# Two-layer decode kernel: 384 more columns of W_q stay on chip, 384 more columns of V are lent out, two loads become one

## The chip, the cores and the metric

The kernel runs on one core of a Trainium2 chip. The metric is device time in microseconds: the median of repeated executions. One execution was also taken apart by the hardware profiler, and all rows below come from that one. A difference of 0.2% is 1.46 us here.

## The reference

Two identical layers run one after the other on a residual stream x of 4 rows and 640 columns (one new token for each of 4 sequences). Each layer is attention over a cache and then a gated MLP, each behind a layer norm:

```python
def attention(x):                       # 32 heads of 128, the last W = 1024 cache entries
    q = (x @ wq).reshape(B, 1, 32, 128)
    p = softmax(q . k_cache[:, :, -1024:, :] * 128 ** -0.5)
    return (p . v_cache[:, :, -1024:, :]).reshape(B, 1, 4096) @ wo

def mlp(x):                             # F = 1728
    gate, up = x @ W_gate, x @ W_up
    return (gate * (gate > 0) * up) @ W_down

x = x + attention(layernorm(x)); x = x + mlp(layernorm(x))     # layer 0
x = x + attention(layernorm(x)); x = x + mlp(layernorm(x))     # layer 1, same weights, same cache
```

Everything is float32. The host only cuts and reorders the arrays; all the arithmetic is on the chip.

## The kernel before

**Layout.** Every operand is laid out over 128 partitions, so that a "column" is one float on each partition (512 bytes in all). There are three long rows of columns in HBM: `heads` (255,744 columns: W_q, K, W_o and V of heads 0 to 26, in the order in which they are used), `kept` (47,360 columns: W_o, W_q, K and V of heads 27 to 31) and `mlp` (25,920 columns). One large buffer `store` (50,624 columns) takes the loads; a second, `first_q` (`HELD` = 4,288 columns), takes the first columns of `heads`, which are the start of W_q.

**What is loaded twice.** Both layers use the same weights and cache, but they do not fit on the chip. `heads` and `mlp` are loaded once in each layer. `kept` is loaded once, at the end of layer 0's attention, and stays for layer 1, which begins with its heads. `first_q` stays as well, so layer 1 loads `heads` from column `HELD` on.

**The plan.** Before any instruction is made, the list `plan` fixes for each load its columns and its place in `store` (`put`, `stretch`, and hand-written lists of sizes such as `gu`, `gu_end` and `wd`). Loads are all issued by SyncE (its queue is SP in the profile), at L216 and L221, strictly in the order of the plan. A load waits on the chip until the last instruction that reads its place in `store` has ended, and the next load waits behind it.

**Groups.** The heads are worked on in nine groups, 0 to 5 of four heads, 6 and 7 of three and 8 of two. Groups 7 and 8 are `kept`. In the loop of `attention`, the step of group g does, in this order on TensorE: the transposes of g's probabilities (L440 into `pp`), the end of group g-1 (L477), the scores of group g+1 (`ps`, L252 through `product`), the projection of group g-1 by W_o (`y`, L252) and the values of group g (`po`, L252). So in the step of group 6 the scores of group 7 stand ahead of the projection of group 5.

**Lent places.** While `kept` lies in `store`, layer 0's MLP still has to be loaded. Three pieces of `kept` are copied away by ScalarE, so that MLP columns can use their places: `AHEAD` (768 columns, into `probs`), `BACK` (1,600 columns, into idle PSUM columns of `ps`, `po` and `yy`) and `AWAY` (1,408 columns, into idle columns of `pp` and of the two `banks`). `BACK` comes back into `store` during layer 1's first scores (L428 to L430), `AWAY` at the end of layer 0's MLP (L610 to L612).

Of the kernel before, what the change touches and what calls it, by code (L numbers as in the profile page):

```python
# [13 lines left out]
B, D, H, DH, W, F = 4, 640, 32, 128, 1024, 1728  # L14
P = 128
KC = D // P
QUARTER = D // 4
# [34 lines left out]
GU0, GU = KC * 3 * P, KC * 4 * 256  # L52
WD0 = GU0 + 3 * GU
TAIL, WD1, WD = WD0 + D, WD0 + D + 2 * QUARTER, 4 * D
MLP = WD1 + 3 * WD
# [2 lines left out]

HELD = 4288
STORE = 50624
FRONT = KEPT * 2 * (D + KV)


AHEAD = KEPT * D, KEPT * D + 768
BACK = FRONT - 2 * KV - 1600, FRONT - 2 * KV
AWAY = BACK[0] - 1408, BACK[0]
HOME = 12992
FIRST, MOST = 32640, 16320  # L70
LAP = 3 * MOST + 1024
# [36 lines left out]
def decode_kernel(ctx: ExitStack, tc: tile.TileContext, x, source, sel, out):  # L108
    nc = tc.nc
# [10 lines left out]
    store = big.tile([P, STORE], F32, name="store")  # L120
# [3 lines left out]
    away = store[:, AWAY[0]:AWAY[1]]  # L124
# [43 lines left out]


    f, z, a, q, k = FRONT, STORE - D, AHEAD[0], AWAY[0], BACK[0]  # L170
    assert STORE - FRONT == 2 * 1280 + 64 + D
    gu = [(z, D), (f, 1280), (f + 1280, 1344), (a, 768), (k, 960), (k + 960, 640), (q, 1408)]
    gu_end = [(f, 1280), (f + 1280, 1280), (f + 2560, D)]
    wd = [(a, D), (k, 960), (k + 960, D), (q, 1280), *gu_end, (a, D), (k, D), (k + D, D)]
    lo = 0
    for to, n in gu + gu + gu_end + wd:
        put(0, "mlp", to, lo, lo + n)
# [2 lines left out]


    lo = HELD
    for to, n in (f, 1280), (f + 1280, 1280), (f + 2560, D + 64), (a, 768), (k, 1600):
        put(1, "heads", to, lo, lo + n)
        lo += n
    to = AHEAD[1]
# [14 lines left out]
    to = stretch(1, hi, last, 0)  # L201
    for lo, hi in (last, near(last + 12800)), (near(last + 12800), heads_end):
        to = put(1, "heads", to if to + hi - lo <= STORE else 0, lo, hi)
    cuts = [0, 7040, 12160, GU0 + 3 * GU, WD1 + WD, MLP - 4 * D, MLP - 2 * D, MLP - D, MLP]
    for lo, hi in zip(cuts, cuts[1:]):
        to = put(1, "mlp", to if to + hi - lo <= STORE else 0, lo, hi)

# [88 lines left out]

    ps = ps_s.tile([P, 2, 512], F32, name="ps")
    pp = ps_p.tile([P, 2, 512], F32, name="pp")
    parked = pp.rearrange("p j n -> p (j n)")[:, 256:896]
    po = ps_o.tile([P, 512], F32, name="po")  # L300
    nc.vector.memset(ps, 0.0)
    nc.vector.memset(po, 0.0)
# [113 lines left out]
    def scores(layer, g):  # L416
        n = len(HEADS[g])
        to = sc[g] = pp if layer and g == order[1][0] else ps
        for i, h in enumerate(HEADS[g]):
            for j in range(2):  # L420
                for b in range(B):
                    lo = (j * B + b) * 512
                    at = SIDE - 1 + SIDE * (B * i + b) - i
                    product(to[32 * b:32 * b + SIDE, j, :], qT[:, at:at + SIDE], *part(layer, "k", h, lo, 512),
                            start=i == 0, stop=i == n - 1, tile_position=(0, 32 * b))
                    part_done(layer, "k", h, lo, 512)
                    if to is pp and k0 + i * KV + lo < HOME + BACK[1] - BACK[0] <= k0 + i * KV + lo + 512:
                        nc.scalar.copy(store[:, HOME:HOME + 1024], ps.rearrange("p j n -> p (j n)"))  # L428
                        nc.scalar.copy(store[:, HOME + 1024:HOME + 1280], po[:, 256:])
                        nc.scalar.copy(store[:, HOME + 1280:HOME + 1600], yy[:, QUARTER:3 * QUARTER])  # L430
        nm[g] = small.tile([P, 1], F32, name="nm", bufs=1)
        nc.vector.tensor_reduce(nm[g], to.rearrange("p j n -> p (j n)"), axis=AX.X, op=ALU.max, negate=True)  # L432

# [8 lines left out]
    def values(layer, g, last=False):  # L442


        n = len(HEADS[g])
        for i, h in enumerate(HEADS[g]):
            t = pT[i % 2]
            to = t[:, GAP:].rearrange("p (c x) -> p c x", c=8)[:, :, :B]
            for j in range(2):
                nc.vector.tensor_copy(to[:, 4 * j:4 * j + 4], pp[:, j].rearrange("p (c x) -> p c x", c=4)[:, :, i:P:32])  # L450
            for c in range(8):
                a = c % 4
                at = GAP + SIDE * B * c - B * i
                product(po[32 * a:32 * a + SIDE * B], t[:, at:at + SIDE * B], *part(layer, "v", h, c * 512, 512),
                        start=i == 0 and c < 4, stop=i == n - 1 and c >= 4, tile_position=(0, 32 * a))
                part_done(layer, "v", h, c * 512, 512)
        if last:
            waits[0] = layer == 0
            fill(1, pp[:, 0])
        nc.scalar.copy(gates, po)  # L460
        if last and layer == 0:
            nc.scalar.copy(po[:, 256:], store[:, BACK[0] + 1024:BACK[0] + 1280])
            nc.scalar.copy(parked, away[:, :640])
            free(*BACK)

    def totals(g):
# [24 lines left out]
    def attention(layer):  # L491
        gs = order[layer]
        rstd = query(layer, gs[0], True, normalized())
        query_out(gs[0], rstd)
        query(layer, gs[1])
        query_turned(gs[0])
        go_on()
        query_out(gs[1], rstd)
        scores(layer, gs[0])
        query(layer, gs[2])  # L500
        softmax(gs[0])
        query_turned(gs[1])
        query_out(gs[2], rstd)
        for before, g, after, then in zip([None] + gs, gs, gs[1:] + [None], gs[2:] + [None] * 2):
            totals(g)
            turned()
            if layer == 0 and after is None:
                nc.scalar.copy(probs[:, QUARTER:QUARTER + 768], store[:, AHEAD[0]:AHEAD[1]])
                nc.scalar.copy(ps.rearrange("p j n -> p (j n)"), store[:, BACK[0]:BACK[0] + 1024])
                nc.scalar.copy(yy[:, QUARTER:3 * QUARTER], store[:, BACK[1] - 320:BACK[1]])  # L510
                free(*AHEAD)
            if before is not None:
                values_turned(before)
            if then is not None and before is not None:
                query(layer, then)
                query_out(then, rstd)
            if after is not None:
                scores(layer, after)
                softmax(after)
            else:  # L520
                table(AF.Sqrt)
            if then is not None:
                query_turned(then)

            if before is not None and not (layer == 0 and after is None):
                project(layer, before)
            values(layer, g, after is None)
        values_turned(gs[-1])
        if layer == 0:
            for i in range(2):  # L530
                nc.scalar.copy(banks[i][:, P:], away[:, 640 + 384 * i:1024 + 384 * i])
            free(*AWAY)
            project(layer, gs[-2])
        fill(1)
        project(layer, gs[-1], True)

    def forward(layer):
# [69 lines left out]
        down(0)  # L607
        hidden(2, h)
        if layer == 0:
            nc.scalar.copy(away[:, :640], parked)  # L610
            for i in range(2):
                nc.scalar.copy(away[:, 640 + 384 * i:1024 + 384 * i], banks[i][:, P:])  # L612
            live[AWAY[0]:AWAY[1]] = [True] * 1408
        down(1)
        down(2, last=True)

# [62 lines left out]
```

## Time and profile before

| | |
|---|---|
| median of 3 runs | 731.91 us (731.81 to 732.6) |
| the profiled execution, its own time | 731.96 us |
| its span, first to last instruction | 730.2 us |
| TensorE busy, mean granted clock | 443.9 us (61%), 0.82 |
| VectorE, ScalarE busy | 76.1 us, 54.5 us |
| queue of the loads, share of the 16 DMA engines | 99.0% |
| moved | 311.17 MB, 426 GB/s over the span |

The span is the part of an execution that the trace covers; the execution's own time is 1.76 us longer. The share of a DMA queue is the time that its packets took, as a share of 16 engines' span. The granted clock is that of TensorE, as a share of 2.4 GHz, and it has two levels, 1.0 and 0.5.

### The profile page before, as it was taken

The numbers are of one execution on the slowest core, as the hardware profiler recorded it, in microseconds if no ns is written. First come the engines' busy times: TensorE is split into PE (matmuls) and PEld (weight loads), VectorE is DVE, ScalarE is ACT, GpSimd is POOL, SyncE is SP. The second block draws the span as 40 slices with busy tenths as digits, with TensorE's granted clock in tenths as the row PEclk, the third lists the DMA queues.
The fourth block names the chain that finished last, engine by engine and source line by source line (L and its number), as shares of the span: only waits on it lengthen the run. The fifth ranks groups of instructions, "written<-read, shape, count | busy, mean of one in ns | idle before, by whom it ended". The sixth has DMA issues, their size and how long they took to land.

```text
span 730.2 us, 8291 instructions
## 1 busy us (share of the span) xinstructions
PE 443.9 (61%) x3776; PEld 147.1 (20%) x3776; DVE 76.1 (10%) x277; ACT 54.5 (7%) x101; POOL 0.2 (0%) x4
## 2 busy tenths in 40 slices
PE   0845665654646565519878896365656556555576
PEld 0211111111111111103344241021111112111233
DVE  1110001010010101002111211001010010101011
ACT  0200000000000000000412210000000000000110
POOL 0000000000000000000000000000000000000000
PEclk9976788877777776759999999677777778878899
DMA  9999999999999999999999999999999999999996
GB/s 409 446 393 446 442 439 437 419 436 439 432 428 429 417 456 424 443 413 429 420 409 396 432 429 446 442 436 424 432 431 443 436 430 423 446 432 432 416 427 286
DMA packets 13290, 311.17 MB, mean 426 GB/s; under 512 B 1476, under 2 KB 1732, under 8 KB 6984
## 3 DMA queue, kind: packets, MB, share of 16 engines
q1 hardware_dynamic: 13104, 310.56, 99.0%
q8 instruction: 29, 0.48, 0.2%
q10 hardware_dynamic: 152, 0.09, 0.1%
q14 instruction: 5, 0.04, 0.0%
HBM read 310.57 MB, written 0.08 MB: 425 GB/s over the span
## 4 chain that ended last, share of the span: by engine, by line
DMA 77%; PE 20%; another core or an unknown queue 1%; issue 1%; DVE 0%; ACT 0%; SPq 0%; DVEq 0%; ACTq 0%
DMA store<-in_heads 60%; PE ps L252 9%; DMA store<-in_kept 8%; DMA store<-in_mlp 8%; PE po L252 5%; PE m L252 2%; PE y L252 1%; PE pp L252 1%; PE pp L440 1%; PE m L411 1%; PE m L477 0%; PE m L468 0%; PE m L349 0%; PE y L379 0%
## 5 line engine op out<-in xcount | busy, mean ns | idle before, releaser
L252 PE MATMUL po<-store,pT 128*16 128x512 f32 (+1 forms) x1026 | 156.0, 716 | 122.4 <-DMA store<-in_heads 117.0
L252 PE MATMUL ps<-store,qT 128*4 128x512 f32 (+3 forms) x996 | 151.0, 687 | 109.5 <-DMA store<-in_heads 87.9
L252 PEld LDWEIGHTS po<-store,pT 128*16 128x16 f32 x1026 | 34.4, 110 | 230.8 <-issue 110.7
L252 PEld LDWEIGHTS ps<-store,qT 128*4 128x4 f32 x996 | 30.0, 93 | 213.2 <-DMA store<-in_heads 98.9
L432 DVE TENSOR_REDUCE nm<-ps 128x1 f32<-128x1024 f32 x17 | 20.8, 1225 | 241.0 <-PE ps L252 241.0
L436 ACT ACTIVATE probs<-ps,nm 128x1024 f32<-128x1024 f32 x17 | 18.9, 1114 | 327.2 <-DVE nm L432 327.2
L252 PE MATMUL m<-store,xT 128*32 128x512 f32 (+4 forms) x150 | 29.0, 580 | 10.5 <-DMA store<-in_heads 10.3
L450 DVE COPY pT<-pp 128x16 f32<-128x16 f32 x128 | 17.2, 169 | 137.5 <-PE po L252 137.5
L460 ACT COPY gates<-po 128x512 f32<-128x512 f32 x18 | 10.5, 586 | 268.3 <-PE po L252 268.3
L252 PE MATMUL y<-store,oT 128*4 128x160 f32 x514 | 22.8, 309 | 9.6 <-DMA store<-in_heads 8.4
L440 PE MATMUL pp<-sel_sb,probs 128*128 128x128 f32 x144 | 20.4, 289 | 0.0
L470 DVE RECIPROCAL r<-m 128x16 f32<-128x16 f32 x18 | 4.6, 258 | 132.2 <-PE m L468 132.2
L440 PEld LDWEIGHTS pp<-sel_sb,probs 128*128 128x128 f32 x144 | 17.9, 151 | 0.0
L252 PE MATMUL pp<-store,xT 128*32 128x256 f32 (+3 forms) x172 | 14.3, 417 | 4.7 <-DMA store<-in_mlp 4.7
L252 PEld LDWEIGHTS y<-store,oT 128*4 128x4 f32 x514 | 12.7, 88 | 17.3 <-DMA store<-in_heads 8.8
L404 DVE TENSOR_SCALAR gates<-m,rstd 128x512 f32<-128x512 f32 (+2 forms) x18 | 12.4, 690 | 24.3 <-PE m L252 24.0
L477 PE MATMUL m<-sel_sb,gates 128*128 128x128 f32 x72 | 11.8, 291 | 1.1 <-ACT gates L460 1.1
L411 PE MATMUL m<-sel_sb,gates 128*128 128x128 f32 x64 | 12.4, 318 | 0.0
L327 PE MATMUL y<-probs,sel_sb 4*4 4x160 f32 x8 | 0.7, 445 | 18.0 <-DMA sel_sb<-in_sel 18.0
L411 PEld LDWEIGHTS m<-sel_sb,gates 128*128 128x128 f32 x64 | 7.7, 157 | 19.2 <-issue 18.8
L252 PE MATMUL y<-store,gates 128*4 128x160 f32 x192 | 9.6, 299 | 2.4 <-DMA store<-in_mlp 2.2
L252 PEld LDWEIGHTS m<-store,xT 128*32 128x32 f32 x150 | 6.2, 116 | 22.0 <-DMA store<-in_heads 12.5
(79 smaller groups left out, 143.5 us busy)
## 6 DMA issues: line engine op xcount, KB each, us to landing
store<-in_heads SPq DMA_DIRECT2D x17, 7936.0 KB, 45.8
store<-in_heads SPq DMA_DIRECT2D x2, 8160.0 KB, 44.5
store<-in_heads SPq DMA_DIRECT2D x2, 8128.0 KB, 35.9
store<-in_heads SPq DMA_DIRECT2D x2, 7968.0 KB, 36.3
store<-in_heads SPq DMA_DIRECT2D x1, 8096.0 KB, 26.3
store<-in_heads SPq DMA_DIRECT2D x1, 7424.0 KB, 44.1
store<-in_heads SPq DMA_DIRECT2D x1, 7360.0 KB, 35.4
store<-in_heads SPq DMA_DIRECT2D x1, 7168.0 KB, 35.1
```

The lines of the kernel that those rows point to most:

```text
L252: nc.tensor.matmul(out[:, a:z], by, t[rows, p:p + z - a], start=start and not a, stop=stop and z == n, **how)
L327: nc.tensor.matmul(y[32 * g:32 * g + B], ident[:B, :B], probs[:B, g * QUARTER:(g + 1) * QUARTER], start=True, stop=True, tile_position=(0, ...
L404: nc.vector.tensor_scalar(gates[:, :len(HEADS[g]) * P], qp.pop(g), rstd, SCALE, op0=ALU.mult, op1=ALU.mult)
L411: nc.tensor.transpose(qt[:, i], gates[:, i * P:(i + 1) * P], ident)
L432: nc.vector.tensor_reduce(nm[g], to.rearrange("p j n -> p (j n)"), axis=AX.X, op=ALU.max, negate=True)
L436: nc.scalar.activation(probs, sc.pop(g).rearrange("p j n -> p (j n)"), AF.Exp, bias=nm.pop(g), accum_out=sums[g])
L440: nc.tensor.transpose(pp[:, c // 4, c % 4 * P:c % 4 * P + P], probs[:, c * P:(c + 1) * P], ident)
L450: nc.vector.tensor_copy(to[:, 4 * j:4 * j + 4], pp[:, j].rearrange("p (c x) -> p c x", c=4)[:, :, i:P:32])
L460: nc.scalar.copy(gates, po)
L470: nc.vector.reciprocal(r[g], so.rearrange("p (b i) -> p i b", b=B)[:, :SIDE])
L477: nc.tensor.transpose(ot[:, 127 * b:127 * b + P], gates[:, b * P:(b + 1) * P], ident)
```

## The change

`HELD` goes from 4,288 to 4,672 columns and `store` from 50,624 to 50,240, so the sum stays. `AWAY` grows by 384 columns at its lower end. Its columns now go to 768 idle columns of `pp` (640 before), 768 of the two `banks` (as before) and 256 of the two `pT` tiles. `pT` has to hold zeros between the probabilities that it carries, so GpSimd clears its first 128 columns after the copy back. The pieces of `BACK` change places among their three homes. The MLP's loads in layer 0 are cut otherwise (same number of columns), and layer 1's first 12,160 MLP columns come in one load, not in 7,040 and 5,120.

```diff
-HELD = 4288
-STORE = 50624
+HELD = 4672
+STORE = 50240
 FRONT = KEPT * 2 * (D + KV)
 AHEAD = KEPT * D, KEPT * D + 768
 BACK = FRONT - 2 * KV - 1600, FRONT - 2 * KV
-AWAY = BACK[0] - 1408, BACK[0]
+AWAY = BACK[0] - 1792, BACK[0]
...
-    gu = [(z, D), (f, 1280), (f + 1280, 1344), (a, 768), (k, 960), (k + 960, 640), (q, 1408)]
-    gu_end = [(f, 1280), (f + 1280, 1280), (f + 2560, D)]
-    wd = [(a, D), (k, 960), (k + 960, D), (q, 1280), *gu_end, (a, D), (k, D), (k + D, D)]
+    gu = [(z, D), (f, 1152), (f + 1152, 1088), (a, 768), (k + 448, 1152), (k - D, 1088), (q, 1152)]
+    gu_end = [(f, 1408), (f + 1408, 1472), (k - 512, 320)]
+    wd = [(a, D), (k, 960), (k + 960, D), (q, 1280), (f, 1280), (f + 1280, 1280), (f + 2560, 320), (k, 320), (a, D),
+          (k + 320, D), (k + 960, D)]
...
     lo = HELD
-    for to, n in (f, 1280), (f + 1280, 1280), (f + 2560, D + 64), (a, 768), (k, 1600):
+    for to, n in (f, 1280), (f + 1280, 1280), (f + 2560, 320), (a, 768), (k, 1600):
...
-    cuts = [0, 7040, 12160, GU0 + 3 * GU, WD1 + WD, MLP - 4 * D, MLP - 2 * D, MLP - D, MLP]
+    cuts = [0, 12160, GU0 + 3 * GU, WD1 + WD, MLP - 4 * D, MLP - 2 * D, MLP - D, MLP]
...
-    parked = pp.rearrange("p j n -> p (j n)")[:, 256:896]
+    parked = pp.rearrange("p j n -> p (j n)")[:, 256:]
...
-            nc.scalar.copy(parked, away[:, :640])
+            nc.scalar.copy(parked, away[:, 1024:])
...
-                nc.scalar.copy(banks[i][:, P:], away[:, 640 + 384 * i:1024 + 384 * i])
+                nc.scalar.copy(banks[i][:, P:], away[:, 256 + 384 * i:640 + 384 * i])
+            for i in range(2):
+                nc.scalar.copy(pT[i][:, :P], away[:, P * i:P * i + P])
...
-            nc.scalar.copy(away[:, :640], parked)
+            nc.scalar.copy(away[:, 1024:], parked)
             for i in range(2):
-                nc.scalar.copy(away[:, 640 + 384 * i:1024 + 384 * i], banks[i][:, P:])
-            live[AWAY[0]:AWAY[1]] = [True] * 1408
+                nc.scalar.copy(away[:, 256 + 384 * i:640 + 384 * i], banks[i][:, P:])
+                nc.scalar.copy(away[:, P * i:P * i + P], pT[i][:, :P])
+                nc.gpsimd.memset(pT[i][:, :P], 0.0)
+            live[AWAY[0]:AWAY[1]] = [True] * (AWAY[1] - AWAY[0])
```

The plan is worked out from these numbers, so sizes and places of loads move elsewhere too. First, SP's queue at the end of layer 0's attention, before: the last loads of `heads` and the first of `kept` (columns are the second number).

```order
L221 DMA store<-in_heads 128x14336
L221 DMA store<-in_heads 128x14720
L221 DMA store<-in_heads 128x14848
L221 DMA store<-in_kept 128x12288
L221 DMA store<-in_kept 128x8192
L221 DMA store<-in_kept 128x6656
L221 DMA store<-in_kept 128x5632
```

The same place after the change:

```order
L222 DMA store<-in_heads 128x14336
L222 DMA store<-in_heads 128x14208
L222 DMA store<-in_heads 128x14848
L222 DMA store<-in_kept 128x12288
L222 DMA store<-in_kept 128x8192
L222 DMA store<-in_kept 128x6656
L222 DMA store<-in_kept 128x5632
```

The second load shown is 512 columns shorter. In both kernels it begins at place 20,736 of `store` and ends with column 240,896 of `heads`; its last place is 35,456 before and 34,944 now. The loads of `kept` keep sizes and places.

Second, ScalarE at the end of layer 0's attention, before: the copies that lend places out (`po`, `pp`, `m` are PSUM; `m` is `banks`).

```order
L460 COPY gates<-po 128x512
L462 COPY po<-store 128x256
L463 COPY pp<-store 128x640
L531 COPY m_109<-store 128x384
L531 COPY m_110<-store 128x384
L357 COPY probs<-y 128x160
```

After the change:

```order
L461 COPY gates<-po 128x512
L463 COPY po<-store 128x256
L464 COPY pp<-store 128x768
L532 COPY m_109<-store 128x384
L532 COPY m_110<-store 128x384
L534 COPY pT_98<-store 128x128
L534 COPY pT_99<-store 128x128
L358 COPY probs<-y 128x160
```

One copy is 128 columns longer and two of 128 columns are new; two such also follow the copies back at the end of layer 0's MLP.

Third, the end of SP's queue, before:

```order
L221 DMA store<-in_heads 128x12672
L221 DMA store<-in_mlp 128x7040
L221 DMA store<-in_mlp 128x5120 x2
L221 DMA store<-in_mlp 128x3520
L221 DMA store<-in_mlp 128x2560
```

After the change:

```order
L222 DMA store<-in_heads 128x12672
L222 DMA store<-in_mlp 128x12160
L222 DMA store<-in_mlp 128x5120
L222 DMA store<-in_mlp 128x3520
L222 DMA store<-in_mlp 128x2560
```

The first two loads of the second MLP are one. Elsewhere one small load is new, so the number of loads into `first_q` and `store` stays at 90.

## Rows read from the trace of the kernel before

**Rows 1.** The page: DMA busy share in 40 slices, and the loads' queue.

```profile
DMA  9999999999999999999999999999999999999996
...
q1 hardware_dynamic: 13104, 310.56, 99.0%
```

**Rows 2.** Windows: length, busy (instructions) by engine PE to POOL, PEclk, DMA share, GB/s.

```profile
3.00:200.00 197.00, 108.16 (x743) 32.14 (x746) 16.84 (x56) 11.32 (x19) 0.00 (x0) 0.80 1.01 435
...
450.00:696.00 246.00, 135.64 (x1015) 40.14 (x1017) 19.42 (x78) 11.03 (x18) 0.00 (x0) 0.78 1.00 433
```

**Rows 3.** The chain that ended last, its end: start, length, what.

```profile
695.92 30.69 DMA store<-in_mlp
...
726.65 0.50 PE y L252 x8
```

**Rows 4.** Timeline of SP, five short stretches: start and length of the issue.

```profile
0.73 0.37 SPq L216 DMA_DIRECT2D first_q<-in_heads  x1
...
298.10 0.33 SPq L221 DMA_DIRECT2D store<-in_kept  x1
...
301.46 0.33 SPq L221 DMA_DIRECT2D store<-in_kept  x1
...
380.80 0.33 SPq L221 DMA_DIRECT2D store<-in_mlp  x1
...
392.11 0.33 SPq L221 DMA_DIRECT2D store<-in_heads  x1
```

**Rows 5.** DMA issues at 0.73, 298.10, 301.46 and 377.51: size, us to landing.

```profile
first_q<-in_heads SPq DMA_DIRECT2D x1, 2144.0 KB, 7.5
...
store<-in_kept SPq DMA_DIRECT2D x1, 4096.0 KB, 37.5
...
store<-in_kept SPq DMA_DIRECT2D x1, 3328.0 KB, 42.0
...
store<-in_mlp SPq DMA_DIRECT2D x1, 640.0 KB, 6.6
```

**Rows 6.** The chain that ended last, 323 to 346 us and before 396.

```profile
325.66 7.96 PE ps L252 x48
...
333.99 1.20 PE y L252 x32
...
388.48 7.07 DMA store<-in_mlp
```

**Rows 7.** DMA queues, packets begun at 0.7 to 1.7 and 1.7 to 2.7 us.

```profile
q10 hardware_dynamic: 3, 0.01, 6.9%
...
q1 hardware_dynamic: 16, 0.27, 105.2%
```

**Rows 8.** DMA packets begun at 332.90 to 333.85 us.

```profile
DMA packets 16, 0.33 MB, mean 343 GB/s; under 512 B 4, under 2 KB 4, under 8 KB 4
```

**Rows 9.** ScalarE's groups by form: busy us, mean ns of one, idle before.

```profile
L531 ACT COPY m<-store 128x384 f32<-128x384 f32 x2 | 0.9, 472 | 0.0
...
L463 ACT COPY pp<-store 128x640 f32<-128x640 f32 x1 | 0.7, 688 | 0.0
```

**Rows 10.** Timeline of TensorE, 707 to 726 us: start, length, what.

```profile
707.41 1.18 PE L252 MATMUL po<-store,xT 128*32 128x128 f32 x27 [0.25 <-DVE xT L363]
...
709.14 2.37 PE L252 MATMUL pp<-store,xT 128*32 128x256 f32 x40
...
716.39 4.05 PE L252 MATMUL pp<-store,xT 128*32 128x256 f32 x40 [2.25 <-DMA store<-in_mlp]
...
721.23 1.27 PE L252 MATMUL y<-store,gates 128*4 128x160 f32 x32
```

**Rows 11.** Windows, 717 to 721 us, columns as in rows 2.

```profile
717.00:719.00 2.00, 2.00 (x24) 1.27 (x20) 0.00 (x0) 0.00 (x0) 0.00 (x0) 0.50 0.98 419
719.00:721.00 2.00, 1.98 (x31) 0.76 (x24) 0.10 (x1) 0.37 (x1) 0.00 (x0) 0.72 1.00 419
```

**Rows 12.** DMA issues at 672.69 us: size, us to landing.

```profile
store<-in_mlp SPq DMA_DIRECT2D x1, 2560.0 KB, 37.5
```

More of the change, by code (lines that the diff above doesn't have):

```diff
@@ L170, in decode_kernel @@
     f, z, a, q, k = FRONT, STORE - D, AHEAD[0], AWAY[0], BACK[0]
-    assert STORE - FRONT == 2 * 1280 + 64 + D
-    gu = [(z, D), (f, 1280), (f + 1280, 1344), (a, 768), (k, 960), (k + 960, 640), (q, 1408)]
-    gu_end = [(f, 1280), (f + 1280, 1280), (f + 2560, D)]
-    wd = [(a, D), (k, 960), (k + 960, D), (q, 1280), *gu_end, (a, D), (k, D), (k + D, D)]
+    assert STORE - FRONT == 2 * 1280 + 320
+    gu = [(z, D), (f, 1152), (f + 1152, 1088), (a, 768), (k + 448, 1152), (k - D, 1088), (q, 1152)]
+    gu_end = [(f, 1408), (f + 1408, 1472), (k - 512, 320)]
+    wd = [(a, D), (k, 960), (k + 960, D), (q, 1280), (f, 1280), (f + 1280, 1280), (f + 2560, 320), (k, 320), (a, D),
+          (k + 320, D), (k + 960, D)]
     lo = 0
@@ L427, in scores @@
                     if to is pp and k0 + i * KV + lo < HOME + BACK[1] - BACK[0] <= k0 + i * KV + lo + 512:
-                        nc.scalar.copy(store[:, HOME:HOME + 1024], ps.rearrange("p j n -> p (j n)"))
-                        nc.scalar.copy(store[:, HOME + 1024:HOME + 1280], po[:, 256:])
-                        nc.scalar.copy(store[:, HOME + 1280:HOME + 1600], yy[:, QUARTER:3 * QUARTER])
+                        nc.scalar.copy(store[:, HOME + 576:HOME + 1600], ps.rearrange("p j n -> p (j n)"))
+                        nc.scalar.copy(store[:, HOME:HOME + 256], po[:, 256:])
+                        nc.scalar.copy(store[:, HOME + 256:HOME + 576], yy[:, QUARTER:3 * QUARTER])
         nm[g] = small.tile([P, 1], F32, name="nm", bufs=1)
@@ L461, in values @@
         if last and layer == 0:
-            nc.scalar.copy(po[:, 256:], store[:, BACK[0] + 1024:BACK[0] + 1280])
-            nc.scalar.copy(parked, away[:, :640])
+            nc.scalar.copy(po[:, 256:], store[:, BACK[0]:BACK[0] + 256])
+            nc.scalar.copy(parked, away[:, 1024:])
             free(*BACK)
@@ L508, in attention @@
                 nc.scalar.copy(probs[:, QUARTER:QUARTER + 768], store[:, AHEAD[0]:AHEAD[1]])
-                nc.scalar.copy(ps.rearrange("p j n -> p (j n)"), store[:, BACK[0]:BACK[0] + 1024])
-                nc.scalar.copy(yy[:, QUARTER:3 * QUARTER], store[:, BACK[1] - 320:BACK[1]])
+                nc.scalar.copy(ps.rearrange("p j n -> p (j n)"), store[:, BACK[1] - 1024:BACK[1]])
+                nc.scalar.copy(yy[:, QUARTER:3 * QUARTER], store[:, BACK[0] + 256:BACK[0] + 576])
                 free(*AHEAD)
```

## The prediction

> **What bounds the kernel now.** I read the page first: the 16 DMA engines show 9 in 39 of 40 slices, and the queue of the loads alone fills 99.0% of them [rows 1]. The windows say at what rate: 433 to 435 GB/s at a share of 1.00 or more, while TensorE is busy for about half of the same stretches [rows 2]. The chain that ended last closes with a load that lands at 726.61 us (695.92 + 30.69) and one short group of matmuls behind it [rows 3]. So the span is the time in which the engines move 311 MB, plus a start and an end of a few us. A byte less is worth its time at 434 GB/s. TensorE, ScalarE and VectorE matter only where a load is issued so late that the queue runs dry, for with the engines full everywhere else such time is never made up.
>
> So for each load I compared two times: when it is issued, and when the load before it lands. Most have 15 us or more between them. The tightest that I found before is the first small load of layer 1, issued at 392.11 while the load ahead lands at 388.48 + 7.07 = 395.55 [rows 4, 6]: 3.1 us of queue are left when its issue ends.
>
> **The bytes saved.** Layer 1 starts loading `heads` at column 4,672, not 4,288. That is 384 columns x 512 bytes = 196,608 bytes, and at 434 GB/s 0.45 us. The kept columns of layer 0 are only moved from one load into another. The number of loads is the same, so what each row of a load costs beyond its bytes stays.
>
> **The load that now comes late.** `store` got shorter by 384 and the plan cut one load of layer 0 by 512 columns (14,720 to 14,208). It still ends with column 240,896 of `heads`, now at place 34,944. W_o of head 20, the first head of group 5, is columns 238,976 to 239,616, so it ends 1,280 places ahead of that: it lies at 33,536 to 34,176 before, and at 33,024 to 33,664 now. The load of 6,656 `kept` columns (V of group 7) goes to 26,880 to 33,536 in both. Before, it just misses W_o, and its last reader is an early V; now its last 512 places are still W_o of head 20, and it has to wait for the fourth matmul of group 5's projection. That projection stands behind the scores of group 7 on TensorE.
>
> What this costs is read at one place. Before, this load (3,328 KB) is issued at 301.46, and the 4,096 KB load ahead of it at 298.10 lands 37.5 us later, at 335.6; the late one itself lands at 343.5 [rows 4, 5]. The chain shows group 7's scores at 325.66, released by the landing of their K, and the projection from 333.99 [rows 6]. The bytes up to here are the same, so these times stay. The 16 matmuls are 32 records in 1.20 us, and the first head's are done about 0.4 us in: the issue moves from 301.5 to 334.4 us. Nothing can be issued meanwhile, since SP is in order and every later load stands behind it; the only data left in the queue are the 4,096 KB load's.
>
> How long the engines then stand still has to be bounded, as no row before shows a dry queue in the middle:
> - *Start of a load into an empty queue.* The first load is the nearest case. Issued at 0.73, it has no packet by 1.7, and 16 packets (one an engine) begin from 1.7 to 2.7 us [rows 4, 7]: 1.0 to 1.9 us after the start of the issue, 1.5 in the mean. For an issue at 334.4 the rows begin from 335.4 to 336.3, in the mean at 335.9.
> - *Where the engines would have been.* They do not finish a load together. In 0.95 us from 332.90 on 12 large packets begin and make up 0.33 MB, 27 KB each [rows 8]: that is the row length of the late load (26.6 KB), not of the one ahead (32.8 KB). So most engines are in it by 333 us. I take 333.1 as the mean.
> - *From above:* 336.3 less 332.2, some 4.1 us. *From below:* by landings, which the last engine sets. The first load lands 7.5 us after its issue [rows 5], and its 2,195,456 bytes take 5.06 us at 434 GB/s, so 2.4 us come on top. Issued at 334.4, 3,407,872 bytes (7.85 us) land at 344.7 instead of 343.5: 1.2 us.
>
> I take the mean over the engines, 335.9 - 333.1 = 2.8 us, since each engine has the same rows to move afterwards and the last of 16 to finish is hardly the one that was last here.
>
> A rule of the skill speaks for less. The Trainium skill ("DMA: Bandwidth & Descriptors", Latency and other measured facts) gives a DMA issued from SP about 600 ns to its first byte. By that, as an estimate, the stream would go on at 335.0, 1.9 us would be lost, and the time would be 733.4. The first load's packets, at 1.0 us and later, do not agree [rows 7].
>
> **The other edits.** ScalarE's copies while lending: 128 more columns in `pp` and two copies of 128. By the rows for 384 columns (472 ns) and 640 columns (688 ns) [rows 9], 128 columns cost some 0.11 us more in a copy and a copy of 128 some 0.25 us: 0.6 us in all, and the two loads that wait for these copies come up to 1.0 us later than before. They have about 7 us of queue ahead of them, as the small MLP loads land 7 us after issue [rows 5, 6]; if that cover were gone, the price would be 1.0 us. The same copies back, and GpSimd's clearing, end several us before layer 1's layer norm or its first values need them. In layer 0's MLP one load of 320 columns now waits for the first matmuls of the last gate tile. The load behind which it stands is at the place of the one that lands at 377.51 + 6.6 = 384.1, and its issue falls where 380.80 stands now [rows 4, 5]: 3 us of queue are left, about the tightest margin of before, so nothing is lost, and if its queue ran dry too, some tenths. Columns that fall in two loads split a few matmuls; TensorE has room.
>
> **The joined load.** It waits for the same values as the second of the two before (issued at 672.69, over 20 us ahead) [rows 12], so the queue does not notice. But TensorE may start the second MLP only when all 12,160 columns are there: where that load landed before, 672.69 + 37.5 = 710.2, and not at 707.41 [rows 10, 12]. On the clock of before, 1.3 us of the first gate tile, 0.5 of layer-norm matmuls and three tiles of 2.37 with 0.5 between them end at 719.6. An idle stretch of 2.25 us made TensorE drop to 1.2 GHz: the granted clock is 0.50 at 717 to 719 and 0.72 over the next 2 us, and the tile that ran in it took 4.05 us [rows 10, 11]. Now the idle stretch is about 3 us; a like drop costs 1.7 us, so the last tile ends at 721.3. Then 0.8 + 3 x 1.27 us of W_down follow, to 726.0, and the last load lands at 726.6. The cover is 0.6 us; it is hidden.
>
> **Sum.** The profiled execution's own time is 731.96 us (span 730.2 and 1.76 around it), 0.05 over the median. 731.96 + 2.8 - 0.45 = 734.3 us.
>
> **The rivals.**
> - *The queue dries up for less.* Only the last engine of the late load counts (1.2 us), or all engines start as soon as the first one did (335.4 - 333.1 = 2.3 us). For it: the end of the span is also a last engine's. Against it: the last here had no reason to be last at the end. 731.96 + 1.2 - 0.45 = 732.7, up to 733.8. The rule of the skill named above lies in between.
> - *No dry queue, not slower.* TensorE would have to reach head 20's projection 2 us sooner, before 332 us, less the time to start. Then only the bytes count: 731.96 - 0.45 = 731.5. The scores run 7.96 us behind a landing that the change does not touch [rows 6], which speaks against it. The same result comes if the saved bytes are all and the overlap of 512 places was misread.
> - *The joined load shows at the end.* If TensorE stays at 1.2 GHz longer than one such stretch, its work passes the last landing. A second stretch costs 1.7 us, of which 0.6 are covered: 1.1 more. With all four tiles at 1.2 GHz (2.6 and three of 4.05 us) they end at 726.5 and W_down at 731.1, 3.9 us behind the end of before. It comes on top: 735.4 to 738.2.
>
> **How the numbers follow.** The forecast has a chance of 0.69 at 734.3 us, by the bounds 1.2 and 4.1 at most 732.7 to 735.6. The smaller dry time has 0.16, no dry queue 0.08, the joined load on top 0.07. With 0.2% (1.46 us, about what a measurement tells from no change) slower begins at 733.37. The forecast is over it for 0.63, the smaller dry time for 0.04, the last rival for 0.06, together 0.73. Faster by over 0.2% needs 1 us more than the bytes give: 0.03. The rest, 0.24, is the same. The range reaches from 732.4 to 735.6: it leaves out the case without a dry queue and most of the last rival.
>
> **What would show it.** In the trace after, the 3,328 KB load is issued near 334.4 us with a projection matmul (`y`) as what it waited for, and lands some 10 us later, at 344.7 or after, not 42.0. The DMA share falls in the slice around 335, and all behind it is later by 2 to 3 us until layer 1's loads give 0.45 back. The MLP of layer 1 begins right with the landing of the joined load, and the last group of matmuls still waits for the last load. I would be wrong if that issue stands near 301 us, if the queue stays full at 335, or if TensorE ends later than 0.6 us behind the last landing.

## The result, and the profile after

The changed kernel takes 735.03 us in the median of 6 runs (734.12 to 735.96), against 732.09 us for the kernel before beside it: a ratio of 1.0039, 95% interval 1.0027 to 1.0051. It is slower by 2.9 us, 0.4%. The profiled execution took 735.43 us with a span of 733.6; the one of before, 731.96 and 730.2.

The page of the kernel after: the DMA busy share and the rate in 40 slices of 18.3 us, and the queue of the loads.

```profile
DMA  9999999999999999998999999999999999999996
GB/s 420 393 443 444 436 441 433 409 443 434 437 447 422 409 447 444 426 428 354 417 419 389 417 426 462 429 437 422 430 444 436 430 428 438 432 432 429 430 423 276
...
q1 hardware_dynamic: 13104, 310.37, 98.6%
```

Beside [rows 1] one slice of the share has an 8, and it is the one in which the rate falls to 354 GB/s: the 19th, 330 to 348 us. The bytes went from 310.56 to 310.37 MB. Far from that place the rate is that of before; windows of after, to be read beside [rows 2]:

```profile
3.00:200.00 197.00, 105.67 (x741) 30.82 (x744) 16.86 (x56) 11.25 (x19) 0.00 (x0) 0.80 1.01 435
450.00:696.00 246.00, 143.74 (x1043) 42.25 (x1041) 21.18 (x85) 12.23 (x20) 0.00 (x0) 0.76 1.00 434
```

SP's timeline of after, two short stretches; the first two loads answer to 298.10 and 301.46 in [rows 4]:

```profile
298.24 0.33 SPq L222 DMA_DIRECT2D store<-in_kept  x1
...
334.56 0.33 SPq L222 DMA_DIRECT2D store<-in_kept  x1
```

The view of waits of after, SP from 297 to 340 us (what it waited for: us in all, times, longest), and three lines of the chain that ended last, in order of time:

```profile
SPq L222 <- PE y L253: 36.0, 1, 36.0
```

```profile
325.73 8.01 PE ps L253 x48
333.75 0.37 PE m L412 x2
334.11 1.20 PE y L253 x32
```

DMA issues of after at 298.24 and at 334.56: size, us to landing.

```profile
store<-in_kept SPq DMA_DIRECT2D x1, 4096.0 KB, 37.5
...
store<-in_kept SPq DMA_DIRECT2D x1, 3328.0 KB, 11.7
```

So the load of 3,328 KB waits 36 us for a projection matmul, is issued 33.1 us later than before and lands at 346.3 (334.56 + 11.7) instead of 343.5. The load ahead of it has landed at 335.7. What the engines did meanwhile stands in the windows, here the same four of before and then of after (columns as in [rows 2]). A load is moved in rows, one packet for each partition (a "row" from here on is such a packet); a window counts a row whole where it begins, so a share can be over 1.00, and the 0.08 below means that two rows begin from 333 to 335 us while earlier ones still run.

```profile
331.00:333.00 2.00, 2.00 (x20) 0.39 (x16) 0.00 (x0) 0.00 (x0) 0.00 (x0) 1.00 1.14 486
333.00:335.00 2.00, 2.00 (x42) 0.95 (x34) 1.30 (x3) 0.00 (x0) 0.00 (x0) 1.00 0.97 419
335.00:337.00 2.00, 2.00 (x28) 0.59 (x24) 0.52 (x6) 1.21 (x2) 0.00 (x0) 1.00 0.99 426
337.00:339.00 2.00, 2.00 (x24) 0.47 (x17) 0.17 (x1) 0.00 (x0) 0.00 (x0) 1.00 0.99 426
```

```profile
331.00:333.00 2.00, 2.00 (x24) 0.39 (x16) 0.00 (x0) 0.00 (x0) 0.00 (x0) 0.95 0.91 393
333.00:335.00 2.00, 2.00 (x39) 0.95 (x34) 1.18 (x2) 0.00 (x0) 0.00 (x0) 1.00 0.08 33
335.00:337.00 2.00, 2.00 (x28) 0.49 (x20) 0.65 (x7) 1.20 (x2) 0.00 (x0) 1.00 0.84 226
337.00:339.00 2.00, 2.00 (x24) 0.59 (x20) 0.17 (x1) 0.00 (x0) 0.00 (x0) 1.00 1.00 426
```

The ten microseconds around the pause as one window, of before and then of after:

```profile
331.00:341.00 10.00, 10.00 (x111) 3.21 (x104) 2.21 (x9) 1.56 (x3) 0.00 (x0) 1.00 1.01 434
331.00:341.00 10.00, 10.00 (x114) 3.10 (x103) 2.08 (x9) 1.41 (x3) 0.00 (x0) 0.99 0.77 301
```

The last two columns are what counts. From the shares, the engines stand idle for 2 x (0.09 + 0.92 + 0.16) = 2.3 us. From the rates the loss is larger: (486 - 393) + (419 - 33) + (426 - 226) = 679 GB/s over 2 us each, at 434 GB/s 3.1 us. The difference lies in the third window: a share of 0.84 at the rate of before would move 360 GB/s, and it moves 226. The engines are at work there, but on rows that take longer, and that is 0.6 us more: in the trace the first 16 rows behind the pause, one for each engine, begin at 335.53 to 336.16 us and take 1.21 to 1.95 us, 1.62 in the mean, where rows of this size take 0.99 otherwise.

The end of the program. The chain of after has these lines near its end, which answer to [rows 3]:

```profile
690.64 39.43 DMA store<-in_mlp
...
730.11 0.50 PE y L253 x8
```

and TensorE's timeline of after reads there, beside [rows 10]:

```profile
713.90 2.14 PE L253 MATMUL po<-store,xT 128*32 128x128 f32 x27 [3.01 <-DMA store<-in_mlp]
...
717.01 2.37 PE L253 MATMUL pp<-store,xT 128*32 128x256 f32 x40
...
727.14 1.27 PE L253 MATMUL y<-store,gates 128*4 128x160 f32 x32 [1.08 <-DMA store<-in_mlp]
...
730.11 0.46 PE L253 MATMUL y<-store,gates 128*4 128x160 f32 x8 [0.32 <-DMA store<-in_mlp]
```

with these windows, beside [rows 11]:

```profile
713.00:715.00 2.00, 1.10 (x18) 1.14 (x21) 0.00 (x0) 0.00 (x0) 0.00 (x0) 0.62 1.00 430
715.00:717.00 2.00, 2.00 (x28) 1.72 (x22) 0.16 (x1) 0.38 (x2) 0.00 (x0) 0.53 0.91 390
717.00:719.00 2.00, 2.00 (x41) 1.20 (x40) 0.28 (x1) 0.19 (x1) 0.00 (x0) 1.00 1.06 449
```

TensorE idles for 3.01 us, starts the second MLP with the landing of the joined load, has a granted clock of 0.62 and 0.53 until 717 (mostly the lower level, 1.2 GHz) and of 1.00 (2.4 GHz) from 717 to 719, and is waiting again when the last load lands.

Last, a stretch of layer 0's MLP and the start of layer 1, first of before and then of after:

```profile
376.00:390.00 14.00, 11.05 (x135) 5.04 (x139) 1.32 (x4) 0.94 (x3) 0.00 (x0) 1.00 1.01 408
376.00:430.00 54.00, 47.78 (x517) 19.67 (x521) 9.47 (x27) 9.30 (x19) 0.00 (x0) 1.00 1.02 418
```

```profile
376.00:390.00 14.00, 10.27 (x120) 4.79 (x124) 2.06 (x7) 1.10 (x3) 0.00 (x0) 1.00 1.01 391
376.00:430.00 54.00, 46.89 (x508) 19.74 (x512) 10.20 (x30) 10.14 (x22) 0.41 (x2) 1.00 1.02 412
```

Over the 54 us the rate is 6 GB/s lower, at 434 GB/s 0.75 us. With 3.06 us at the dry queue (331 to 341 us move 434 GB/s before and 301 after) and 0.45 us of bytes saved, the account is 3.06 + 0.75 - 0.45 = 3.4 us; the two profiled executions differ by 3.47. The prediction had nothing for the 0.75, so this was the open question.

### The profile page after: what moved, and what is told of

Same layout as the page of the kernel before. It is cut to its first block, busy times and chain, and to the rows that moved or that the text cites. A ratio compares the mean times of both kernels' runs of the same rounds, so it can differ in the third digit from the quotient of the medians.

```text
span 733.6 us, 8294 instructions
## 1 busy us (share of the span) xinstructions
PE 447.7 (61%) x3776; PEld 149.0 (20%) x3776; DVE 76.1 (10%) x277; ACT 55.5 (8%) x105; POOL 0.6 (0%) x6
## 2 busy tenths in 40 slices
DMA packets 13290, 310.98 MB, mean 424 GB/s; under 512 B 1476, under 2 KB 2244, under 8 KB 7112
## 3 DMA queue, kind: packets, MB, share of 16 engines
q1 hardware_dynamic: 13104, 310.37, 98.6%
HBM read 310.37 MB, written 0.08 MB: 423 GB/s over the span
## 4 chain that ended last, share of the span: by engine, by line
DMA 77%; PE 21%; issue 1%; DVE 0%; ACT 0%; SPq 0%; DVEq 0%; ACTq 0%
DMA store<-in_heads 60%; PE ps L253 10%; DMA store<-in_mlp 9%; DMA store<-in_kept 8%; PE po L253 6%; PE m L253 1%; PE y L253 1%; PE pp L253 1%; PE m L412 1%; PE pp L441 0%; PE m L478 0%; SPq L222 0%; PE m L469 0%; PE m L342 0%; PE m L350 0%
## 5 line engine op out<-in xcount | busy, mean ns | idle before, releaser
L253 PE MATMUL po<-store,pT 128*16 128x512 f32 x1030 | 156.5, 712 | 132.3 <-DMA store<-in_heads 124.7
L253 PE MATMUL ps<-store,qT 128*4 128x512 f32 (+3 forms) x996 | 156.7, 703 | 107.1 <-DMA store<-in_heads 84.7
L253 PE MATMUL po<-store,xT 128*32 128x256 f32 (+3 forms) x148 | 10.4, 359 | 5.2 <-DMA store<-in_mlp 4.9
L253 PE MATMUL pp<-store,xT 128*32 128x256 f32 (+3 forms) x172 | 11.9, 369 | 2.4 <-DMA store<-in_mlp 2.4
```

What stands on the lines that cost most here:

```text
L253: nc.tensor.matmul(out[:, a:z], by, t[rows, p:p + z - a], start=start and not a, stop=stop and z == n, **how)
```

## The experiments

Two theories. The first: the late load of V is the whole loss, and the small loads of the MLP cost nothing, as the prediction had it. The second: there is another loss in layer 0's MLP, hidden in the first result by the size of the other. Twelve kernels were run. All compute the whole of the reference. The times are medians of 4 to 11 runs, ratios are to the kernel before on the same chip (731.96 to 732.13 us).

**1. The change without the late load** (`e1`): one load of `kept` ends 512 columns earlier, so that it misses W_o of head 20.

```
-    put(0, "kept", k0, k0, k1, v0, v0 + 6656, v1, v1 + KV, v1 + 7168, FRONT)
+    put(0, "kept", k0, k0, k1, v0, v0 + 6144, v1, v1 + KV, v1 + 7168, FRONT)
```

> The changed kernel with one number altered: the load of V of group 7 ends at place 33,024 instead of 33,536, so it no longer covers W_o of head 20, and the 512 columns go into the load behind it. Theory (the late load is the whole loss): the load is issued near 301 us again, the queue stays full at 335, and 2.3 us of standing still and 0.6 us of slow first rows go; with the saved 0.45 us the time is 731.5 to 732.2, not slower than before (732.09). Rival (the joined load, the longer copies or the new cuts of the first MLP's loads cost the time): it stays at 734 to 735.

Measured: 733.34 us, ratio 1.0025 (1.0014 to 1.0036). The load is issued at 301.60 again and nothing is lost at 331 to 341 us, but 1.3 us over the kernel before remain, though 0.45 us of bytes are saved: some 1.7 us are lost elsewhere. That lies between the numbers of the theory and of the rival. Windows of this kernel:

```profile
331.00:341.00 10.00, 10.00 (x114) 3.86 (x107) 2.25 (x9) 1.79 (x3) 0.00 (x0) 1.00 1.02 437
376.00:390.00 14.00, 9.51 (x116) 4.31 (x117) 1.32 (x4) 0.73 (x2) 0.00 (x0) 1.00 0.97 363
376.00:430.00 54.00, 46.04 (x497) 19.29 (x498) 9.46 (x27) 9.77 (x21) 0.41 (x2) 1.00 1.01 399
```

399 against 418 GB/s over 54 us are 2.4 us in this execution (its own time, 733.83, was half a us over its median). The first theory falls. In this kernel the longer copies and the joined load are still there too; experiments 4 and 5 bear on what they cost.

**2. The late load alone** (`e2`): the same cut put the other way into the kernel before.

```
-    put(0, "kept", k0, k0, k1, v0, v0 + 6656, v1, v1 + KV, v1 + 7168, FRONT)
+    put(0, "kept", k0, k0, k1, v0, v0 + 7168, v1, v1 + KV, v1 + 7168, FRONT)
```

> The kernel before with one number altered: the load of V of group 7 ends at 34,048 instead of 33,536, 512 columns taken from the load behind it, so that it has to wait for head 20's projection. Nothing else of the change is in it. Theory: the same dry queue at 333 to 336 us, about 2.9 us in the mean engine and up to 3.5 us at the last landing: 735.0 to 735.6. Rival (the wait alone is harmless): 732.1.

Measured: 734.44 us, ratio 1.0034 (1.0022 to 1.0046), 2.4 us more than before and 0.6 under the range expected; the profiled execution took 735.46, 1.0 over the median. SP and the windows of this kernel:

```profile
334.79 0.33 SPq L221 DMA_DIRECT2D store<-in_kept  x1
```

```profile
331.00:341.00 10.00, 10.00 (x112) 2.91 (x105) 2.00 (x8) 1.21 (x2) 0.00 (x0) 0.97 0.77 300
376.00:390.00 14.00, 11.06 (x132) 5.35 (x132) 2.06 (x7) 1.10 (x3) 0.00 (x0) 1.00 1.02 416
```

The dry queue of after (0.77 and 301 GB/s) is here without any other edit of the change, and the MLP's stretch is untouched.

**3. More and less of it** (`e3`, `e6`). In the kernel before, the same V comes in one load with its rest, `v0 + 6656` left out of the list; or only 1,024 columns come early.

```
-    put(0, "kept", k0, k0, k1, v0, v0 + 6656, v1, v1 + KV, v1 + 7168, FRONT)
+    put(0, "kept", k0, k0, k1, v0, v1, v1 + KV, v1 + 7168, FRONT)                      # e3
+    put(0, "kept", k0, k0, k1, v0, v0 + 1024, v0 + 7168, v1, v1 + KV, v1 + 7168, FRONT)    # e6
```

> A larger dose in the kernel before: V of group 7 comes as one load of 12,288 columns instead of 6,656 and 5,632, and so waits for the values of group 6, which end near 337.1 us. Theory: the queue is empty from about 333 until 1.5 us after 337.1, 5.5 us, and 0.6 us are lost in slow first rows: 737.5 to 738.5. Rival (a fixed price for a restart, whatever its length): about 735, as in the change.

> The kernel before with the late V load, but the first 1,024 of its columns come as a load of their own at the old early time, so the queue holds 1.2 us more when the rest has to wait. Theory (the price of the dry queue grows with its length and has a fixed part for slow first rows): 1.3 us of standing still and 0.6 us of slow first rows, 733.5 to 734.2. Rival (a fixed price for a restart): 734.5, as with the whole load late.

Measured: `e3` 738.67 us, ratio 1.0091 (1.0077 to 1.0104), 0.2 over the range expected; `e6` 733.03 us, ratio 1.0013 (1.0004 to 1.0023), 0.5 under it. Both are far from the rival, a fixed price for a restart. The loads are issued at 336.17 and 334.24. Windows of `e3`, then of `e6`:

```profile
331.00:341.00 10.00, 10.00 (x111) 3.84 (x103) 2.25 (x9) 1.79 (x3) 0.00 (x0) 1.00 0.62 239
...
349.00:360.00 11.00, 5.50 (x28) 1.26 (x32) 0.35 (x2) 0.00 (x0) 0.00 (x0) 0.53 0.93 400
```

```profile
331.00:341.00 10.00, 10.00 (x113) 3.40 (x106) 2.25 (x9) 1.75 (x3) 0.00 (x0) 1.00 0.92 365
```

With a share of 1.01, 0.92, 0.77 and 0.62 over these 10 us (idle 0, 0.8, 2.3 and 3.8 us) the median is 0, 0.9, 2.4 and 6.6 us over that of before. The windows are of one execution each, and those of `e6`, `e2` and `e3` were 0.9, 3.4 and 5.6 us over; their rates over the 10 us lose 1.6, 3.1 and 4.5. The pause has its price at every size, so it is the cause of what `e2` lost. The last step is more than the pause: in `e3` TensorE, which then waits for V, goes to a granted clock of 0.53 from 349 to 360 us, and the rate there is 400 GB/s where the kernel before has 419.

**4. The joined load alone** (`e4`).

```
-    cuts = [0, 7040, 12160, GU0 + 3 * GU, WD1 + WD, MLP - 4 * D, MLP - 2 * D, MLP - D, MLP]
+    cuts = [0, 12160, GU0 + 3 * GU, WD1 + WD, MLP - 4 * D, MLP - 2 * D, MLP - D, MLP]
```

> The kernel before with the joined load of 12,160 columns alone. It has one load less, 8 rows an engine. Theory: TensorE starts the second MLP 3 us later and at the low clock and catches up before the last landing; 731.9 to 732.3, the same. Rival (the joined load shows at the end): 733 or more, with TensorE's last group over 0.6 us behind the last landing.

Measured: 732.14 us, ratio 1.0001 (0.9991 to 1.001). Its TensorE timeline:

```profile
710.62 2.14 PE L252 MATMUL po<-store,xT 128*32 128x128 f32 x27 [3.29 <-DMA store<-in_mlp]
...
713.79 3.67 PE L252 MATMUL pp<-store,xT 128*32 128x256 f32 x40
...
717.73 2.37 PE L252 MATMUL po<-store,xT 128*32 128x256 f32 x40
...
725.47 1.16 PE L252 MATMUL y<-store,gates 128*4 128x160 f32 x24 [0.28 <-DMA store<-in_mlp]
726.92 0.46 PE L252 MATMUL y<-store,gates 128*4 128x160 f32 x8 [0.29 <-DMA store<-in_mlp]
```

One tile runs slow (3.67 instead of 2.37 us), and the last matmuls still wait for the last load: it costs nothing.

**5. The second loss: two parts of the cut** (`e5`, `e12`, `e10`). In the changed kernel two things of the MLP's cut are new. A load of 320 columns waits for the last gate tile and all later loads stand behind it; and the loads of gate and up have other sizes, so that one of 1,088 columns (11,840 to 12,928 of `mlp`) lies over the border at 12,160 between the last two gate tiles. `e5` takes `e1` and gives the 320 columns a place that is free earlier:

```
-    gu_end = [(f, 1408), (f + 1408, 1472), (k - 512, 320)]
-    wd = [(a, D), (k, 960), (k + 960, D), (q, 1280), ...
+    gu_end = [(f, 1408), (f + 1408, 1472), (a, 320)]
+    wd = [(a + 320, 448), (k, 960), (k + 960, D), (q, 1472), ...
```

`e12` takes `e1` and only cuts the gate and up loads otherwise, so that one ends at 12,160 (two loads more); `e10` does both, and cuts the loads of W_down behind them to fit (three loads more than the change). The edit that `e12` and `e10` share:

```
-    gu = [(z, D), (f, 1152), (f + 1152, 1088), (a, 768), (k + 448, 1152), (k - D, 1088), (q, 1152)]
+    gu = [(z, D), (f, 1152), (f + 1152, 1088), (a, 768), (k + 448, 1152), (k + 128, 320), (q + 960, 960), (q, 960)]
```

> The run with the early V load left 1.3 us over before, and its trace shows why: in layer 0's MLP a load of 320 columns waits for the last gate tile at 381.5 us with 2.9 us of queue left, and five loads stand behind it, where before the queue held 5.8 us. This kernel has the early V load and puts those 320 columns, and the 448 behind them, where AHEAD was lent, which is free earlier. One load behind still waits for the last gate tile, with some 0.9 us more of queue. New theory (the thin queue is the second loss): part of it comes back, 732.2 to 733.0. Rival (the second loss is elsewhere): 733.3, as without the move.

> The changed kernel with V of group 7 early, and of the cut without the second loss only the gate and up loads (borders on the borders of the gate tiles); the 320 columns wait for the last gate tile as in the change. If that wait is the second loss, 733.0 to 733.5 us, as with V early alone (733.34). If the borders inside the gate tiles are the loss, 732.2 to 732.6 us.

> The changed kernel with V of group 7 issued early (no dry queue), and the MLP's loads in layer 0 cut so that their borders fall on the border between the gate tiles and no load of 320 columns waits in front of others for the last gate tile; no load over 1,600 columns. Three loads more. If the late V and the wait of the 320 columns are the two losses, the 0.45 us of saved bytes are left over: 731.5 to 732.1 us, and 376 to 390 us moves about 400 GB/s. If what costs is something that this cut keeps (the longer lending copies, the pieces that wait for them, the number of small loads), it stays at 732.6 to 733.3 us as when only the 320-column load was moved.

Measured, with `e1` for comparison:

| kernel | 320 columns wait | a load over 12,160 | us | ratio, 95% interval |
|---|---|---|---|---|
| `e1` | yes | yes | 733.34 | 1.0025 (1.0014 to 1.0036) |
| `e5` | no | yes | 732.78 | 1.0011 (1.0002 to 1.0021) |
| `e12` | yes | no | 732.73 | 1.0011 (1.0002 to 1.002) |
| `e10` | no | no | 732.23 | 1.0001 (0.9992 to 1.001) |

By the medians each of the two edits is worth about half a us, and with both the loss over before is gone. The intervals of neighbours in the table overlap; only the whole step from `e1` to `e10` (1.1 us) is clear of them. `e12` lay between the two numbers that were expected of it, which speaks against one edit being the whole; `e10` came 0.1 over its first range. That the border as such is the cause is not shown, though the two expectations name it: the kernel before has a load over 12,160 as well (640 columns, 12,032 to 12,672) and loses nothing, and all four kernels of the table keep one over the first border, at 1,920 (1,792 to 2,880). The recut changes sizes and number of the loads too. The number of small rows alone is not the cause: `e10` has 2,804 packets under 2 KB and `e1` 2,244, and `e10` is faster. Windows of `e10`, to be read beside those of `e1`, and its next stretch, with that of before last:

```profile
376.00:390.00 14.00, 10.49 (x122) 5.44 (x123) 1.32 (x4) 0.73 (x2) 0.00 (x0) 0.88 1.02 405
376.00:430.00 54.00, 47.76 (x516) 21.03 (x520) 9.47 (x27) 9.77 (x21) 0.41 (x2) 0.97 1.02 411
390.00:400.00 10.00, 9.38 (x142) 4.75 (x143) 1.38 (x5) 3.44 (x10) 0.41 (x2) 1.00 0.97 349
```

```profile
390.00:400.00 10.00, 8.83 (x127) 3.87 (x125) 1.77 (x5) 3.24 (x8) 0.00 (x0) 1.00 1.01 383
```

411 GB/s over the 54 us against 399 in `e1` and 418 before. TensorE's granted clock from 376 to 390 us is 0.88 here and 1.00 in `e1`, so the stretch is not the same otherwise. And `e10` is not the kernel before with fewer bytes: of the 0.45 us saved nothing shows in its time. What its profile still loses lies at 390 to 400 us, where layer 1's first loads begin; why there was not tried.

**6. The wait put into the kernel before** (`e9`, `e11`). There a load of 640 columns (`e9`) or of 320 (`e11`) is given a place that the last gate tile still reads; gate and up loads stay as they were. Only the line of `gu_end` is shown below; the places of the loads behind it change too, in both layers, which makes one load more in `e9` and six in `e11` (14,154 packets in its page, 13,434 in that of `e9`, 13,290 before: 144 for each load more), not the four that its expectation says.

```
-    gu_end = [(f, 1280), (f + 1280, 1280), (f + 2560, D)]
+    gu_end = [(f, 1280), (f + 1280, 1280), (k + 960, D)]                # e9
+    gu_end = [(f, 1408), (f + 1408, 1472), (k + 960, 320)]              # e11
```

> The kernel before, with only one thing of the change: in layer 0's MLP a load of 640 columns waits for the first matmuls of the last gate tile (near 381 us) with the loads behind it in the queue, instead of a load whose place is free earlier; V of group 7 stays early. Bytes the same, one load more in layer 1. If the second loss is this wait and the thin queue after it, the stretch from 376 to 390 us moves about 363 to 385 GB/s instead of 408, and the time is 733.2 to 733.8 us. If the wait is covered by what is left in the queue, as the prediction had it (three us left, nothing lost), and the second loss in the changed kernel has another cause, it is 732.0 to 732.3 us.

> The kernel before, V of group 7 early, the gate and up loads as they were; only the last gate tile's end is cut as in the changed kernel: 1,408 + 1,472 + 320 columns, and the 320 wait for the first matmuls of the last gate tile, with 2.9 us of queue ahead of them. Bytes the same, four small loads more. If a wait with so little queue costs more the smaller the load that waits (a 640-column load cost 0.2 us), the time is 733.0 to 733.8 us. If the second loss of the changed kernel comes from its gate and up loads, whose borders lie inside the gate tiles, the time is 732.1 to 732.7 us.

Measured: `e9` 732.34 us, ratio 1.0004 (0.9995 to 1.0013); `e11` 732.60 us, ratio 1.001 (1.0001 to 1.0019). In `e9` the load is issued at 380.86 us and the load ahead lands at 384.2, as much queue as in `e1`, and it costs 0.2 us and not the 1.1 to 1.7 that the theory said. In `e11` it costs 0.6 (interval 0.1 to 1.4), less than the 1.0 expected at least, with six loads more. Windows of `e9`, then of `e11`:

```profile
376.00:390.00 14.00, 10.66 (x130) 4.80 (x130) 1.32 (x4) 0.73 (x2) 0.00 (x0) 1.00 0.99 385
...
376.00:390.00 14.00, 11.06 (x128) 4.72 (x128) 1.32 (x4) 0.74 (x2) 0.00 (x0) 1.00 0.99 380
```

The rate does fall, from 408 to 385 and 380 GB/s, as the theory of the thin queue said for `e9`; but from 390 to 400 us the two move 403 and 400 where before has 383, and over 376 to 430 us 415 and 416 against 418. A low rate in 14 us is therefore not yet a loss. So the wait alone explains 0.2 to 0.6 us by the medians; the rest of the second loss comes with what the change does besides, most likely the recut of the gate and up loads.

**7. Two attempts that made it worse** (`e7`, `e8`). `e7` is `e5` with the sizes 960 and 640 of the kernel before and one load of 1,792 columns (a load still lies over 12,160, from 11,648 to 12,288); `e8` is `e7` with V late again as in the change.

```
-    gu = [(z, D), (f, 1152), (f + 1152, 1088), (a, 768), (k + 448, 1152), (k - D, 1088), (q, 1152)]
+    gu = [(z, D), (f, 1152), (f + 1152, 1088), (a, 768), (k, 960), (k + 960, 640), (q, 1792)]
```

> The changed kernel with both losses mended: the V load ends at 33,024, and the first MLP's loads in layer 0 are cut as in the kernel before (960, 640 and now 1,792 columns in BACK and AWAY), so that the loads behind the gate tiles wait for the tile before the last. The saved columns, the longer copies and the joined load stay. Theory: only the saved 0.45 us is left of the change, 731.4 to 732.0 against 732.07 before. Rival (something else in the change costs time): 732.5 or more.

> As the one with both losses mended, but with the V load late as in the change. If the two losses simply add, the late load costs 2.4 us here as it did in the kernel before: 734.0 to 734.4. If the pause at 335 us gives the thin queue of the MLP some of its stock, as the difference between the changed kernel (735.0) and the early V load (733.3) suggests, the same 734.0 to 734.4 comes out and the changed kernel lies only some 0.8 us above it, not 1.3.

Measured: `e7` 733.45 us, ratio 1.0022 (1.0013 to 1.003), the rival's case; `e8` 737.30 us, ratio 1.0073 (1.0059 to 1.0087), 2.9 over the range expected. TensorE's timeline of `e7`, then windows of `e8`:

```profile
372.41 0.62 PE L253 MATMUL pp<-store,xT 128*32 128x256 f32 x2 [1.51 <-DMA store<-in_mlp]
```

```profile
375.00:380.00 5.00, 5.00 (x42) 2.73 (x45) 0.74 (x3) 0.37 (x1) 0.00 (x0) 0.66 0.99 389
380.00:385.00 5.00, 3.31 (x57) 1.94 (x48) 0.66 (x2) 0.37 (x1) 0.00 (x0) 1.00 0.97 298
385.00:390.00 5.00, 3.31 (x34) 1.19 (x28) 0.00 (x0) 0.00 (x0) 0.00 (x0) 0.53 1.01 398
```

The large load is whole later, and TensorE waits 1.51 us for it where the longest wait of `e1` from 366 to 390 us is 0.93. That this makes `e7` slow is argued and not shown: the execution that was profiled, 732.59 us, was the shortest of its eleven. The five longest (734.05 us and more) have a mean granted clock of 0.809 to 0.813, the six others 0.815 to 0.824, so more of TensorE's time at the lower clock goes with the longer time there. With V late as well (`e8`) the granted clock goes to 0.66 and 0.53 in stretches in which the change has 1.00, and the rate to 298 GB/s. What the pause costs therefore depends on what follows it: 2.4 us in `e2` and 1.7 in the change (735.03 less 733.34), which is no clear difference, but 3.9 in `e8` over `e7`.

## Why the prediction held, point by point

The forecast of 734.3 us was 0.7 below the median, the median lies inside the range that was given, and the sign was right; but one step was wrong. That the number came so near is in part luck: the 2.8 us for the dry queue are above the 2.4 that `e2` measures, and the loss in the MLP is missing, so the two errors work against each other.

- **The late load** was right in mechanism and place. Expected: issue at 334.4 behind a projection matmul; measured 334.56 with a wait of 36.0 us for `y`. Expected landing: 344.7 or later; measured 346.3.
- **2.8 us for the dry queue.** Measured 3.1 by the rates of this execution and 2.4 by the median of `e2` alone (3.4 by its profiled execution). The sum fits, its make-up less: the engines stand idle for 2.3 us, the case that the prediction had put among the rivals, and the rows right after the pause are slow, 0.6 to 0.7 us that its mean did not have. Its own [rows 7] had shown them: 16 rows in 105.2% of 16 engines' 1 us are 1.05 us for a row of 17 KB, and the rows behind these take 0.65. The start of the rows after the issue, bounded by the first load at 1.0 to 1.9 us, held: 1.0 to 1.6 us (335.53 to 336.16), 335.7 in the mean where 335.9 was expected. The Trainium skill ("DMA: Bandwidth & Descriptors", Latency and other measured facts) gives about 600 ns to the first byte. This trace does not agree: the first row begins 0.97 us after the start of the issue, and the 1.9 us that the prediction's estimate by that figure would have lost are less than the 2.3 idle here.
- **"3 us of queue are left, ... so nothing is lost, and if its queue ran dry too, some tenths": this step failed.** The stretch was read right (the load of 320 columns waits for the last gate tile, in the change until 383.87 us) and so was the margin (the load ahead lands 3.25 us later), its price was not: the term was put at nothing. `e1`, which has all of the change but the late V, is 1.27 us over before in spite of 0.45 us of bytes, so some 1.7 us are lost. Cutting the MLP's loads in another way (`e10`) gives 1.1 of these back, about half by the place of the 320 columns, which the prediction named, and half by the recut of the gate and up loads, which it dismissed with "columns that fall in two loads split a few matmuls". Which property of that recut counts, and where the last 0.6 go, is open. Both had been judged by whether one load comes before the queue is empty. In the changed kernel, where the pause stands ahead of it, the profile shows 0.75 us of this loss and not 1.7. Why the two losses do not add up fully (2.4 and 1.3 over before, 2.9 together) is open; the intervals of about 0.8 us on each leave room for chance.
- **The bytes saved**, 0.45 us, were moved less (310.37 against 310.56 MB), but no run shows them in the time by themselves.
- **The longer copies while lending** held: the load that waits for the last of them is issued at 366.82 us, 6.8 us before the load ahead lands, and up to 376 us `e1` moves as much as the kernel before (419 and 418 GB/s from 344 on).
- **The joined load** was hidden, as predicted: `e4` measures nothing, TensorE begins with the landing (710.62, expected 710.2), one stretch of low clock follows, and the last load still ends it. The cover of 0.6 us was about right: in `e4` TensorE waits 0.28 and 0.29 us before its last two groups, 0.57 in all. In the change, where no whole tile ran slow (2.37 us at 717.01), it waits 1.08, 0.24 and 0.32.
- **The rivals**: no dry queue is refuted by the windows, the joined load at the end by `e4`. The smaller dry time was nearest to the idle time itself, but not to the time of the kernel.

No kernel beat the one before; the best of the changed ones, `e10`, equals it.

## What to carry to other kernels

Where the DMA queue is the bound, a planner that shifts places by a few hundred columns can make one load overlap a buffer that is read much later; list, for every load, what its place holds and who reads that last, before and after. Then look at the margins of all loads that follow, and do not call a margin of 3 us safe in a stretch of small loads without trying it: two edits that each leave the queue non-empty cost about half a us each here. Undo the parts of such a change one by one and both together: the largest loss covered a second one here, and the second one had more than one part.

## What the runs showed of the hardware that was not expected

- After a pause of the queue the first rows are slow: at a share of 0.84 the engines moved 226 GB/s at 335 to 337 us, and at 0.87 in `e2` 229, where a share of 0.99 moves 426. That is 0.6 to 0.7 us on top of the idle time. It does not grow with the row: the first 16 rows take 1.62 us in the mean instead of 0.99 in the change (26.6 KB), 1.74 instead of 1.07 in `e2` (28.7 KB) and 2.48 instead of 1.82 in `e3` (49.2 KB). Why was not tried.
- A stretch of small loads loses rate with engines that are hardly ever idle: `e1` has a share of 0.97 from 376 to 390 us and moves 363 GB/s, where the kernel before has 1.01 and 408. The changed cut has more small rows (2,244 packets under 2 KB in the whole program, 1,732 before), but their number alone does not decide: `e11` has 3,236 and moves 380 GB/s there, `e10` has 2,804 and moves 405.
- Waits of TensorE of about the same length met different clocks: 1.51 us in `e7` at a granted clock that stays 1.00, and a like one in `e8`, after a stretch in which TensorE was busy for 1.32 of 3 us, at 0.66. Two runs do not say what decides.
